# Float16 parts with power-of-two scales in place of float32r parts in a gated MLP

## The chip, the cores and the metric

The kernel runs on one core of a Trainium2 chip. The metric is the device time of one execution in microseconds. Of three runs of the kernel before, the median is 4073.93 us (4071.32 to 4078.27).

## The reference

Three stages follow each other; all data are float32, except that the gated MLP's weights come as float64.

```python
X = np.fft.rfft(x, axis=1)                      # x: 8 sequences x 3072 x 256
Yr = Xr @ w_r - Xi @ w_i + b_r ; Yi = Xr @ w_i + Xi @ w_r + b_i
Y = softshrink(Yr) + 1j * softshrink(Yi)
y = np.fft.irfft(Y, n=3072, axis=1)             # 24576 tokens x 256
z = (sigmoid(y @ w_gate) * (y @ w_val)) @ w_out # 256 -> 1536 -> 256
e = argmax(z @ w_gate8)                         # one of 8 experts per token
out = gate_weight * (relu(z @ w1[e]) @ w2[e])   # 256 -> 1024 -> 256
```

## The kernel before, in words

P1 (lines 84 to 409) transforms one sequence at a time: 256-point transforms as products on TensorE, the 3- and 4-point ones on VectorE (dft3, dft4), the complex mix and the softshrink, and back. The result y goes to DRAM with the features on partitions, in pieces of 128 x 512 (yo, line 406).

P2 (lines 495 to 762) takes y in 48 chunks of 512 tokens, six to a batch (a sequence). A chunk is loaded and split into a high part yhi and a low part ylo (split). A float32 product is made of three products of parts: high by high, high by low, low by high. For each f of 12 groups of 128 hidden features, gvmm issues 12 products of 512 columns into two PSUM tiles gv (six for the gate, six for the value); glu makes the sigmoid (ScalarE), the product p (VectorE), its high part ghi (ScalarE) and its low part glo (VectorE); zmm issues 12 products of 264 columns that add to z (256 outputs, and 8 columns for the choice of the expert, the weights of which prep multiplies into w_out). The z products of a step run behind the gate and value products of the next (pend). There are 48 x 12 = 576 such steps. After 12 of them, route scales the rows of z, chooses the expert and scatters the rows to a table in DRAM.

The parts of y, of p and of the weights are float32r: a high part is a rounded copy, a low part is the rest. The weights arrive as the words of float64 numbers: fetch starts their DMAs once a given value of P1 exists, decode makes float32 of them with integer operations on VectorE and splits them (lines 559 to 584).

The first sequence has the chip to itself. From then on the generator of the next sequence, batch(b + 1), is advanced between the steps of chunk after chunk: nst is the number of its pieces per batch, and they are spread evenly over the first 70 of 72 steps. A list scheduler then sets each engine's order; an engine runs its instructions in that order. Eight products, a maximum and a split for each piece of the experts' weights are woven in the same way (WPrep).

P3 (lines 765 to 994) computes the experts on tiles of 256 sorted rows. Its parts are float16 with a power of two per row and per weight matrix, and again three products stand for one: up (line 918) and down (line 943), each of 256 columns.

## Time and profile before

| | |
|---|---|
| median of three runs | 4073.93 us |
| span of the profiled execution | 4067.2 us |
| TensorE busy | 3994.1 us (98%) |
| VectorE busy | 2443.0 us (60%) |
| ScalarE busy | 1616.1 us (40%) |
| GpSimd busy | 419.6 us (10%) |

For the profiled execution the page gives its span, from the first to the last instruction, and no time around it. A busy time counts each moment once. Products on TensorE overlap, so the mean duration of one is longer than the distance from one to the next; the chain of waits gives a run of products with its count and the time until the next piece, and so their spacing. PE is TensorE's products, PEld its weight loads, DVE is VectorE, ACT ScalarE, POOL GpSimd.

### The profile page before, as it was taken

How to read it: one execution, taken by the hardware profiler on the slowest of the kernel's cores; microseconds unless marked ns; L12 is line 12 of the kernel's file. 1: busy time of each engine (PE TensorE's matmuls, PEld its weight loads, DVE VectorE, ACT ScalarE, POOL GpSimd, SP SyncE). 2: the span in 40 equal slices, each digit the busy share in tenths (PEclk: the TensorE clock that was granted, in tenths of full speed). 3: DMA queues.
4: the chain of work that ended last, by engine and by line, in shares of the span. 5: the costliest groups of instructions: out<-in, count | busy, mean ns of one | idle time of the engine just before them, and what ended most of it. 6: DMA issues, size and time to landing. Idle time of an engine off the chain costs nothing.

```text
span 4067.2 us, 70179 instructions
## 1 busy us (share of the span) xinstructions
PE 3994.1 (98%) x27260; PEld 3533.1 (87%) x27260; DVE 2443.0 (60%) x5820; ACT 1616.1 (40%) x3056; POOL 419.6 (10%) x422
## 2 busy tenths in 40 slices
PE   7899999999999999999999999999999999999998
PEld 5788888888888888888888888888888888888887
DVE  6979768867875886687578568744442222222222
ACT  3545344334544444443344334433333333333332
POOL 1000000000000100000000000000011111111111
PEclk9899999999999999999999999999999999999999
DMA  5311421321252133103101210220032444442442
GB/s 182 112 57 39 143 69 36 108 92 65 68 187 77 68 103 119 37 17 107 42 22 44 87 40 21 85 81 22 11 103 63 122 132 135 132 132 70 116 130 46
DMA packets 289488, 338.00 MB, mean 83 GB/s; under 512 B 153773, under 2 KB 231390, under 8 KB 284928
## 3 DMA queue, kind: packets, MB, share of 16 engines
q1 hardware_dynamic: 267536, 272.70, 23.3%
q0 software_dynamic: 21616, 60.78, 4.2%
q8 instruction: 216, 3.54, 0.4%
q14 instruction: 120, 0.98, 0.1%
HBM read 338.33 MB, written 98.98 MB: 108 GB/s over the span
## 4 chain that ended last, share of the span: by engine, by line
PE 92%; DMA 3%; DVE 2%; issue 2%; ACT 0%; SPq 0%; POOL 0%; POOLq 0%; DVEq 0%; ACTq 0%
PE gv L644 37%; PE zps L671 19%; PE ph L918 12%; PE po L943 12%; PE p1ps L210 5%; PE p1ps L272 2%; DMA u<-A 1%; PE p1ps L394 1%; PE p1ps L194 1%; PE p1ps L393 1%; DMA A<-A 1%; DMA ca<-in_cA 0%; PE eps L943 0%; DMA u<-in_moe_w 0%; PE rps L724 0%
## 5 line engine op out<-in xcount | busy, mean ns | idle before, releaser
L644 PE MATMUL gv<-yhi,w 128*128 128x512 f32 x4608 | 1559.0, 399 | 1.5 <-DVE p L659 1.0
L644 PEld LDWEIGHTS gv<-yhi,w 128*128 128x128 f32 x4608 | 864.6, 188 | 187.5 <-issue 3.0
L644 PE MATMUL gv<-ylo,w 128*128 128x512 f32 x2304 | 909.1, 395 | 0.0
L671 PE MATMUL zps<-w,ghi 128*128 128x264 f32 x4608 | 867.3, 285 | 0.1
L671 PEld LDWEIGHTS zps<-w,ghi 128*128 128x128 f32 x4608 | 751.5, 188 | 49.8 <-ACT ghi L661 0.5
L928 DVE SCALAR_TENSOR_TENSOR hh<-ph,hh 128x512 f16<-128x512 f32 x388 | 268.4, 692 | 731.3 <-ACT hh L927 725.6
L659 DVE TENSOR_TENSOR p<-gv,p 128x512 f32<-128x512 f32 x576 | 396.1, 688 | 487.1 <-PE gv L644 472.6
L671 PE MATMUL zps<-w,glo 128*128 128x264 f32 x2304 | 655.2, 285 | 0.9 <-DVE glo L663 0.9
L658 ACT ACTIVATE p<-gv 128x512 f32<-128x512 f32 x576 | 344.7, 598 | 682.3 <-PE gv L644 661.3
L661 ACT CAST ghi<-p 128x512 fp32r<-128x512 f32 x576 | 357.0, 620 | 588.3 <-DVE p L659 575.4
L943 PE MATMUL po<-wb,hh 128*128 128x256 f16 x4656 | 524.0, 273 | 0.0
L918 PE MATMUL ph<-xT,wb 128*128 128x256 f16 x4656 | 524.0, 273 | 0.0
L943 PEld LDWEIGHTS <-hh 128*128 128x128 f16 x4800 | 470.4, 98 | 59.8 <-issue 4.5
L918 PEld LDWEIGHTS <-wb 128*128 128x128 f16 x4800 | 469.6, 98 | 54.3
L644 PEld LDWEIGHTS gv<-ylo,w 128*128 128x128 f32 x2304 | 433.8, 188 | 78.8
L663 DVE TENSOR_TENSOR glo<-p,ghi 128x512 fp32r<-128x512 f32 x576 | 396.6, 688 | 174.9 <-ACT ghi L661 171.8
L756 POOL DMA_INDIRECT zs<-zr,di x192 | 209.7, 1092 | 2720.8 <-issue 1089.3
L671 PEld LDWEIGHTS zps<-w,glo 128*128 128x128 f32 x2304 | 433.6, 188 | 1.2 <-DVE glo L663 1.1
L927 ACT ACTIVATE hh<-ph 128x512 f16<-128x512 f32 x388 | 232.0, 598 | 283.3 <-PE ph L918 282.5
L953 POOL DMA_INDIRECT out<-ot,tk x200 | 194.9, 974 | 841.6 <-ACT ot L952 832.3
L952 ACT ACTIVATE ot<-po,gs 128x256 f32<-128x256 f32 x194 | 92.1, 475 | 409.1 <-PE po L943 409.1
L210 PE MATMUL p1ps<-wmix,hl 128*128 128x256 f32 x1512 | 196.4, 281 | 0.0
(227 smaller groups left out, 3342.0 us busy)
## 6 DMA issues: line engine op xcount, KB each, us to landing
wb<-wz SPq DMA_DIRECT2D x104, 2048.0 KB
u<-in_moe_w SPq DMA_DIRECT2D x64, 512.0 KB
u<-in_x SPq DMA_DIRECT2D x96, 256.0 KB
y<-yo SPq DMA_DIRECT2D x96, 256.0 KB
y<-y SPq DMA_DIRECT2D x48, 512.0 KB
wz<-u SPq DMA_DIRECT2D x32, 512.0 KB
ca<-in_cA SPq DMA_DIRECT2D x96, 128.0 KB
gc<-in_gC SPq DMA_DIRECT2D x48, 256.0 KB
```

What stands on the lines that cost most here:

```text
L210: nc.tensor.matmul(o, lhsT=lh[:, x, dc], rhs=w[:, wp], start=n == 0, stop=n == 5)
L644: nc.tensor.matmul(ps, lhsT=self.w[f // 4, i, dc][:, wp, f % 4 * 128 : f % 4 * 128 + 128], rhs=yy[:, dc], start=n == 0, stop=n == 5,)
L658: nc.scalar.activation(p, ps[0], AF.Sigmoid)
L659: nc.vector.tensor_tensor(p, ps[1], p, ALU.mult)
L661: nc.scalar.copy(ghi, p)
L663: nc.vector.tensor_tensor(glo, p, ghi.bitcast(F32), ALU.subtract)
L671: nc.tensor.matmul(zps[s][:, : D + NE], lhsT=g[gg][:, sl], rhs=self.w[f // 4, 2, f % 4 // 2][:, f % 2, wp], start=f == 0 and n == 0, stop= ...
L756: i = nc.gpsimd.indirect_dma_start(out=self.zs, out_offset=bass.IndirectOffsetOnAxis(ap=di[:, s : s + 1], axis=0), in_=zw[:, s], in_offset ...
L918: nc.tensor.matmul(ps[:, j], lhsT=w[:, dc * 2 + wp, fc * 128 : fc * 128 + 128], rhs=xT[:, xl * 2 + dc], start=n == 0, stop=n == 5,)
L927: nc.scalar.activation(hh[:, 0, gs2], ps, AF.Relu)
L928: nc.vector.scalar_tensor_tensor(hh[:, 1, gs2], ps, 0.0, hh[:, 0, gs2], ALU.max, ALU.subtract)
L943: nc.tensor.matmul(po, lhsT=hh[:, hl, fc, s * 128 : s * 128 + 128], rhs=w[:, q + wp, k : k + 256], start=n == 0, stop=n == 23,)
```

## The change

The parts in the gated MLP become float16. Before they are split, y is multiplied by a power of two per chunk and the weights by one per matrix. For y, each piece is searched for its largest magnitude as it is written (see); after each third of the inverse transform, of spreads the maximum over the partitions with a transpose and a product and makes the power of two and its inverse. For the weights, wscales does the same over all 18 raw tiles, on the high words of the float64 numbers, before the first is split. The scales are taken out again in the sigmoid's scale, in constants, and in the routing's scales.

```diff
@@ P1.batch, behind the DMA of a piece of y
+                    self.scales.see(q, eh, yf)
                     yield
+            yield from self.scales.of(b, a)
...
+def p2s15(nc, out, P):
+    v = nc.vector
+    v.tensor_scalar(P, P, 16 << 23, 253 << 23, ALU.max, ALU.min)
+    v.tensor_scalar(out[0], P, -1, 268 << 23, ALU.mult, ALU.add)
+    v.tensor_single_scalar(out[1], P, 14 << 23, ALU.subtract)
+
+def spread_max(nc, pool, psum, ident, ones, m, n, name):
+    v = nc.vector
+    ps = psum()
+    nc.tensor.transpose(ps[:n, :128], m, ident)
+    mx = pool.tile([n, 1], F32, tag=name + "x", name=name + "x")
+    v.tensor_reduce(mx, ps[:n, :128], AX.X, ALU.max)
+    dg = pool.tile([n, n], F32, tag=name + "d", name=name + "d")
+    v.tensor_scalar_mul(dg, ident[:n, :n], mx)
+    yield
+    ps = psum()
+    nc.tensor.matmul(ps[:, :n], lhsT=ones[:n, :], rhs=dg, start=True, stop=True)
+    yield ps[:, :n]
+
+class Scales:
...
+    def see(self, q, eh, yf):
...
+        self.nc.vector.tensor_reduce(
+            self.ym[:, q % 2, eh : eh + 1], yf, AX.X, ALU.max, apply_absolute_value=True
+        )
+
+    def of(self, b, a):
...
+        g = spread_max(nc, self.pool, self.pst, self.p2.ident, self.p2.ones, m, 4, "ys")
+        next(g)
+        yield
+        ps = next(g)
+        am = self.pool.tile([128, 2], F32, tag="yam", name="yam")
+        v.tensor_reduce(am, ps.rearrange("p (q h) -> p q h", h=2), AX.X, ALU.max)
...
+        v.tensor_single_scalar(P, P, EXPM, ALU.bitwise_and)
+        p2s15(nc, (sI[:, 0], sI[:, 1]), P)
...
+    def consts(self, c):
+        t = self.pool.tile([128, 4], F32, tag="ct", name="ct", bufs=3)
+        self.nc.vector.tensor_scalar_mul(t, self.p2.kt, self.sc[c][1])
+        return t
...
+    def wscales(self):
...
+        for (q, i, j), t in self.raw.items():
+            n = i * 6 + q * 2 + j
+            h = t.rearrange("p (k t) -> p k t", t=2)[:, :, 1].bitcast(F32)
+            v.tensor_reduce(wm[:, n : n + 1], h, AX.X, ALU.max, apply_absolute_value=True)
...
+        g = spread_max(nc, self.ep, self.pst, self.ident, self.ones, wm, 19, "mw")
...
@@ decode
-            w = self.w[key] = self.wtile(key, [128, 2, 512], F32R)
+            w = self.w[key] = self.wtile(key, [128, 2, 512], F16)
...
-        nc.scalar.copy(hi, Av)
-        v.tensor_tensor(lo, Av, hi.bitcast(F32), ALU.subtract)
+        s = self.sw[:, key[1] : key[1] + 1]
+        nc.scalar.activation(hi, Av, AF.Copy, scale=s)
+        v.scalar_tensor_tensor(lo, Av, s, hi, ALU.mult, ALU.subtract)
...
@@ prep
+        self.wscales()
+        yield
         for q in range(3):
...
@@ split
+        self.yhi = self.yp.tile([128, 2, 512], F16, tag="yhi", name="yhi", bufs=2)
+        self.ylo = self.yp.tile([128, 2, 512], F16, tag="ylo", name="ylo", bufs=2)
+        self.ct[c] = self.scales.consts(c)
+        s = self.scales.sc[c][0]
         for h in range(2):
-            nc.scalar.copy(self.yhi[:, h], self.y32[:, h])
-            nc.vector.tensor_tensor(self.ylo[:, h], self.y32[:, h], self.yhi[:, h].bitcast(F32), ALU.subtract)
+            nc.scalar.activation(self.yhi[:, h], self.y32[:, h], AF.Copy, scale=s)
+            nc.vector.scalar_tensor_tensor(
+                self.ylo[:, h], self.y32[:, h], s, self.yhi[:, h], ALU.mult, ALU.subtract
+            )
...
@@ glu
-        nc.scalar.activation(p, ps[0], AF.Sigmoid)
-        nc.vector.tensor_tensor(p, ps[1], p, ALU.mult)
-        ghi = self.fp.tile([128, 512], F32R, tag="ghi", name="ghi")
+        nc.scalar.activation(p, ps[0], AF.Sigmoid, scale=self.ct[c][:, 0:1])
+        nc.vector.scalar_tensor_tensor(p, ps[1], 2.0**-23, p, ALU.mult, ALU.mult)
+        ghi = self.fp.tile([128, 512], F16, tag="ghi", name="ghi")
         nc.scalar.copy(ghi, p)
-        glo = self.fp.tile([128, 512], F32R, tag="glo", name="glo")
-        nc.vector.tensor_tensor(glo, p, ghi.bitcast(F32), ALU.subtract)
+        glo = self.fp.tile([128, 512], F16, tag="glo", name="glo")
+        nc.vector.tensor_tensor(glo, p, ghi, ALU.subtract)
...
@@ build
-        if k == 55:
+        if k == 34:
             p2.fetch(p1.A[2][:, 0, 0, 0, 0:1])
-    for _ in range(6):
+    for _ in range(7):
         next(prep)
...
-            steps, nst = 0, 118
+            steps, nst = 0, 124
```

The order of TensorE where the first chunk begins. Before, the first two gate and value products (gv, line 644) stand among the inverse transforms of the first sequence (p1ps, lines 397 and 398):

```order
L397 MATMUL p1ps<-gc,u 128x128
L398 MATMUL p1ps<-gc,A_86 128x128
L397 MATMUL p1ps<-gc,u 128x128
L398 MATMUL p1ps<-gn,A_86 128x128
L644 MATMUL gv<-yhi,w_1034 128x512
L644 MATMUL gv<-ylo,w_1034 128x512
L397 MATMUL p1ps<-gc,u 128x128
L398 MATMUL p1ps<-gc,A_86 128x128
```

In the changed kernel, where gv is at line 753, the last inverse transforms (lines 398 and 399) are followed by the pair for the last scale of y (transpose of ym, product with ysd), the pair for the weights (mwm, mwd), and the products that join the expert choice to w_out (lines 705 and 710):

```order
L399 MATMUL p1ps<-gc,A_86 128x128
L398 MATMUL p1ps<-gc,u 128x128
L399 MATMUL p1ps<-gn,A_86 128x128
L453 MATMUL pps<-ident,ym 4x128
L460 MATMUL pps<-ysd,ones 128x4
L453 MATMUL pps<-ident,mwm 19x128
L460 MATMUL pps<-mwd,ones 128x19
L705 MATMUL pps<-ident,u 128x128 x4
L710 MATMUL pps<-wg_481,wt 128x8 x4
L705 MATMUL pps<-ident,u 128x128 x4
L753 LDWEIGHTS w_1142
L753 MATMUL gv<-yhi,w_1142 128x512
```

All gate and value products have moved behind the inverse transforms and the scale pairs.

The order of VectorE in the first sequence's mix. Before, between the values of frequency 128 (h, line 338) and the next dft3 (lines 173 and 174):

```order
L338 TENSOR_TENSOR h_376<-A_85,h_376 128x4
L338 TENSOR_TENSOR h_376<-A_86,h_376 128x4
L313 TENSOR_TENSOR hl<-A_85,hl 128x256
L232 TENSOR_TENSOR A_86<-u 128x4x128
L314 SCALAR_TENSOR_TENSOR hl<-A_85,hl 128x256
L173 TENSOR_TENSOR u<-A_85,A_86 128x516
L174 TENSOR_TENSOR u<-A_85,A_86 128x516
```

In the changed kernel, where these are lines 339, 174 and 175, with the maxima over the raw weight tiles (mwm, line 635):

```order
L339 TENSOR_TENSOR h_379<-A_86,h_379 128x4
L635 TENSOR_REDUCE mwm<-w_441 128x1
L635 TENSOR_REDUCE mwm<-w_443 128x1
L635 TENSOR_REDUCE mwm<-w_445 128x1
L635 TENSOR_REDUCE mwm<-w_447 128x1
L635 TENSOR_REDUCE mwm<-w_449 128x1
L314 TENSOR_TENSOR hl<-A_85,hl 128x256
L635 TENSOR_REDUCE mwm<-w_451 128x1
L233 TENSOR_TENSOR A_86<-u 128x4x128
L315 SCALAR_TENSOR_TENSOR hl<-A_85,hl 128x256
L174 TENSOR_TENSOR u<-A_85,A_86 128x516
L175 TENSOR_TENSOR u<-A_85,A_86 128x516
```

Six of the 18 maxima stand here; two, five and five stand at three other places of the mix.

The order of VectorE in the main loop, near the end of a batch. Before, with p (line 659), glo (line 663), a piece of y (yo, lines 402 and 403) and a maximum for the experts' weights (wm):

```order
L659 TENSOR_TENSOR p<-gv,p 128x512
L663 TENSOR_TENSOR glo<-p,ghi 128x512
L402 TENSOR_TENSOR yo<-p1ps,od 128x2x128
L403 TENSOR_TENSOR yo<-p1ps,od 128x2x128
L402 TENSOR_TENSOR yo<-p1ps,od 128x2x128
L403 TENSOR_TENSOR yo<-p1ps,od 128x2x128
L467 TENSOR_REDUCE wm<-u 128x1
L659 TENSOR_TENSOR p<-gv,p 128x512
L663 TENSOR_TENSOR glo<-p,ghi 128x512
```

In the changed kernel, at such a place (p is line 769, glo 773, yo 403 and 404):

```order
L403 TENSOR_TENSOR yo<-p1ps,od 128x2x128
L404 TENSOR_TENSOR yo<-p1ps,od 128x2x128
L365 MEMSET c_11618 12x2
L475 TENSOR_REDUCE ym<-yo 128x1
L455 TENSOR_REDUCE ysx<-pps 4x1
L457 TENSOR_SCALAR ysd<-ident,ysx 4x4
L769 SCALAR_TENSOR_TENSOR p<-gv,p 128x512
L534 TENSOR_REDUCE wm<-u 128x1
L773 TENSOR_TENSOR glo<-p,ghi 128x512
L488 TENSOR_REDUCE yam<-pps 128x2
L492 TENSOR_SCALAR yam<-yam 128x2
L444 TENSOR_SCALAR yam<-yam 128x2
```

Behind the two instructions of a piece of y now comes its maximum (ym), and behind every fourth piece the chain of a scale (ysx, ysd, yam, then ysc).

## Rows read from the trace of the kernel before

**Rows 1.** Page, busy us of each engine, share of the span, instructions.
```profile
PE 3994.1 (98%) x27260; PEld 3533.1 (87%) x27260; DVE 2443.0 (60%) x5820; ACT 1616.1 (40%) x3056; POOL 419.6 (10%) x422
```
**Rows 2.** Stretches: us, busy PE, PEld, DVE, ACT, POOL, granted clock, DMA, GB/s.
```profile
0.00:141.60 141.60, 96.59 (x525) 76.54 (x526) 105.24 (x257) 54.13 (x97) 15.06 (x30) 0.87 0.53 173
...
1965.49:2325.37 359.88, 359.88 (x2184) 319.26 (x2183) 256.00 (x632) 151.73 (x298) 24.54 (x24) 1.00 0.17 52
...
2997.00:4067.20 1070.20, 1051.82 (x9616) 941.65 (x9614) 306.82 (x663) 336.98 (x610) 198.72 (x204) 0.99 0.40 109
```
**Rows 3.** Waits of PE from 150 to 2985 us: total us, times, longest.
```profile
PE p1ps L394 <- DMA A<-A: 5.3, 7, 1.6
PE zps L671 <- DVE glo L663: 0.9, 1, 0.9
```
**Rows 4.** Chain of waits, last batch: start us, us, run of products.
```profile
2780.28 2.80 PE gv L644 x12
2783.08 1.46 PE zps L671 x12
...
2791.62 1.49 PE zps L671 x12
```
**Rows 5.** Chain of waits in the experts' stage.
```profile
3304.32 5.24 PE ph L918 x48
3309.56 5.24 PE po L943 x48
```
**Rows 6.** Groups, weight loads: count, then busy us and mean ns, idle.
```profile
L644 PEld LDWEIGHTS gv<-ylo,w 128*128 128x128 f32 x2304 | 433.8, 188 | 78.8
...
L918 PEld LDWEIGHTS <-wb 128*128 128x128 f16 x4800 | 469.6, 98 | 54.3
```
**Rows 7.** Groups on DVE and ACT.
```profile
L659 DVE TENSOR_TENSOR p<-gv,p 128x512 f32<-128x512 f32 x576 | 396.1, 688 | 487.1 <-PE gv L644 472.6 <-issue 6.6 <-ACT p L658 5.4
L928 DVE SCALAR_TENSOR_TENSOR hh<-ph,hh 128x512 f16<-128x512 f32 x388 | 268.4, 692 | 731.3 <-ACT hh L927 725.6 <-issue 5.7
L658 ACT ACTIVATE p<-gv 128x512 f32<-128x512 f32 x576 | 344.7, 598 | 682.3 <-PE gv L644 661.3 <-issue 20.1 <-ACT A L279 0.9
L695 DVE TENSOR_REDUCE am<-z 128x4 f32<-128x1024 f32 x48 | 58.3, 1214 | 0.6 <-ACT z L682 0.6
L226 ACT ACTIVATE u<-p1ps,nlam 128x512 f32<-128x512 f32 x12 | 8.2, 688 | 10.9 <-PE p1ps L196 10.9
L434 DVE TENSOR_SCALAR sc<-sc 128x4 int32<-128x4 int32 x48 | 8.0, 167 | 0.0
```
**Rows 8.** Timeline of DVE, two instructions back to back: start us, us.
```profile
59.65 0.69 DVE L173 TENSOR_TENSOR u<-A,A 128x516 f32<-128x516 f32 x1
60.26 0.69 DVE L174 TENSOR_TENSOR u<-A,A 128x516 f32<-128x516 f32 x1
```
**Rows 9.** Chain of waits near 487 us, the routing's small products.
```profile
486.95 0.22 PE rps L724 x2
```
**Rows 10.** Stretches: two chunks; columns as in rows 2.
```profile
330.00:394.90 64.90, 64.90 (x406) 58.33 (x405) 61.23 (x157) 32.10 (x65) 4.60 (x4) 1.00 0.13 41
...
998.40:1062.80 64.40, 64.40 (x402) 57.84 (x402) 56.74 (x143) 33.27 (x62) 6.08 (x4) 1.00 0.22 72
```
**Rows 11.** First stage: timelines of DVE and POOL; waits of DVE before 141.6 us.
```profile
45.79 0.69 DVE L319 TENSOR_TENSOR hl<-A,hl 128x512 fp32r<-128x512 f32 x1
70.87 1.10 POOL L555 DMA_DIRECT2D w<-in_moe_w_gate  x2 [56.01 <-DVE w L552]
...
DVE hl L313 <- ACT hl L311: 5.6, 2, 3.8
...
DVE A L230 <- ACT u L227: 3.9, 2, 3.2
```
**Rows 12.** Chain of waits where the first chunk begins.
```profile
141.85 0.47 PE gv L644 x2
...
146.49 1.16 PE gv L644 x5
```

More of the change, by code (lines that the diff above doesn't have):

```diff
@@ L90, in __init__ @@
         self.psum, self.ps_tag = psum, ps_tag
+        self.scales = None
         self.cp = ctx.enter_context(tc.tile_pool(name="p1c", bufs=1, side="right"))
@@ L405, in batch @@
                         nc.scalar.copy(yo, ps)
[L406 to L408 removed]
+                    yf = yo.rearrange("p j h k -> p (j h k)")
+                    nc.sync.dma_start(out=self.y[b, eh, :, q * 512 : q * 512 + 512], in_=yf)
+                    self.scales.see(q, eh, yf)
                     yield
+            yield from self.scales.of(b, a)
 NE = 8
@@ L436, in p2s, with __init__ @@
     v.tensor_single_scalar(P, P, 1 << 23, ALU.subtract)
+def p2s15(nc, out, P):
[16 more added lines that the diff above has]
+class Scales:
+    def __init__(self, ctx, tc, p2, pst):
+        self.nc, self.p2, self.pst = tc.nc, p2, pst
+        self.pool = ctx.enter_context(tc.tile_pool(name="scl", bufs=1))
+        self.sc, self.ct = {}, {}
+    def see(self, q, eh, yf):
+        if q % 2 == 0 and eh == 0:
+            self.ym = self.pool.tile([128, 2, 2], F32, tag="ym", name="ym", bufs=2)
+        self.nc.vector.tensor_reduce(
+            self.ym[:, q % 2, eh : eh + 1], yf, AX.X, ALU.max, apply_absolute_value=True
+        )
+    def of(self, b, a):
+        nc = self.nc
+        v = nc.vector
+        m = self.ym.rearrange("p q h -> p (q h)")
+        g = spread_max(nc, self.pool, self.pst, self.p2.ident, self.p2.ones, m, 4, "ys")
[4 more added lines that the diff above has]
+        v.tensor_reduce(am, ps.rearrange("p (q h) -> p q h", h=2), AX.X, ALU.max)
+        s = self.pool.tile([128, 2, 2], F32, tag="ysc", name="ysc", bufs=8)
+        sI = s.bitcast(I32)
+        P = am.bitcast(I32)
+        v.tensor_single_scalar(P, P, EXPM, ALU.bitwise_and)
+        p2s15(nc, (sI[:, 0], sI[:, 1]), P)
+        for j in range(2):
+            c = b * 6 + 2 * a + j
+            self.sc[c] = s[:, 0, j : j + 1], s[:, 1, j : j + 1]
+        yield
[3 more added lines that the diff above has]
+        return t
 class WPrep:
@@ L508, in __init__ @@
         self.cp = cpool
-        self.raw, self.w = {}, {}
+        self.scales = Scales(ctx, tc, self, self.pst)
+        self.raw, self.w, self.ct = {}, {}, {}
         self.yp = e(tc.tile_pool(name="yp", bufs=1))
@@ L588, in prep @@
         v = nc.vector
+        self.wscales()
+        yield
         for q in range(3):
@@ L707, in route @@
         ex = ep.tile([128, 2, 4, NE], F32, tag="ex", name="ex")
-        nc.scalar.activation(ex[:, 0], dl, AF.Sigmoid)
-        nc.scalar.activation(ex[:, 1], dl, AF.Sigmoid, scale=-1.0)
+        ct = self.ct.pop(c)
+        nc.scalar.activation(ex[:, 0], dl, AF.Sigmoid, scale=ct[:, 2:3])
+        nc.scalar.activation(ex[:, 1], dl, AF.Sigmoid, scale=ct[:, 3:4])
         t = ep.tile([128, 4, NE], F32, tag="t", name="t")
@@ L750, in route @@
         v.reciprocal(sm, sm)
-        v.tensor_tensor(zw.bitcast(F32)[:, :, D], sm, sc[:, 1], ALU.mult)
+        v.scalar_tensor_tensor(zw.bitcast(F32)[:, :, D], sm, ct[:, 1:2], sc[:, 1], ALU.mult, ALU.mult)
         v.scalar_tensor_tensor(zw[:, :, D + 1], di, 0, self.tok[:, c * 4 : c * 4 + 4], ALU.mult, ALU.add)
```

51 lines of the change are left out of this document (36 added, 15 removed).

## The prediction

> **What bounds the kernel now.** I read the page's busy times first: TensorE is busy for 3994.1 of 4067.2 us, no other engine for more than 60% [rows 1]. Then the busy time by stage. Before 141.6 us the first sequence runs alone, and TensorE is busy for 96.6 us of it; a whole batch of the gated MLP, 360 us, has no gap on TensorE at all, while VectorE is busy for 256 of it; the experts' stage from 2997 us on is as full [rows 2]. The waits of TensorE between 150 and 2985 us confirm it: six groups, of which the reader sees the two largest, sum to 8.5 us [rows 3]. So in the gated MLP, which the change edits, time is what TensorE's instructions take, one after the other, and an edit of the other engines counts only where it makes TensorE wait. In the first 142 us that is the other way round.
>
> **The matrix products.** A step f issues 12 gate and value products of 512 columns, 2.80 us, then 12 products of 264 columns into z, 1.46 us, or 1.49 in some rounds [rows 4]. That is 233.3 and 122 ns each, with float32r operands. The experts' stage shows float16 products with a weight load each, as the change makes them: 48 of 256 columns take 5.24 us, 109.2 ns each [rows 5]. No row shows float16 at 512 or 264 columns, so I bound it. In proportion to 256 columns, 512 take 218.3 ns and 264 take 112.6. If instead a fixed part stands beside the columns, as between float32r's two sizes (slope (233.3 - 122) / 248 = 0.449 ns, fixed part 3.5 ns), then 512 columns take 2 x 109.2 - 3.5 = 214.9 ns and 264 take 112.5. I take 216 and 112.6: the truth should lie between two methods so close. A run of 12 goes from 2.80 to 2.59 us and from 1.465 to 1.35, over 576 steps 121 + 66 us less; with 1.46 as the usual z run it is 63, so 184 us. By the two bounds and the two z runs: 165 to 198.
>
> What could take this back is the weight load. It takes 188 ns beside float32r and 98 ns in float16 [rows 6]. In the experts' stage 98 ns hide under 109 ns, so under 112.6 and 216 they should hide as well.
>
> TensorE gets 24 small pairs more (a transpose of four columns, a product with four columns), three per batch. The nearest row is a float32 pair of the routing, 0.22 us [rows 9]; 24 x 0.2 = 4 us, 3 of each 24 pairs in the first stage. Each second product needs VectorE's maximum and diagonal of the first; the order puts about ten products of the MLP between them in the main loop, which cover two small VectorE instructions.
>
> **VectorE and ScalarE in the main loop.** Replaced instructions cost the same: a scalar_tensor_tensor of 512 columns that writes float16 takes 692 ns, the tensor_tensor 688 [rows 7]. The sigmoid gets its scale from a tile; with an operand from a tile a ScalarE activation out of PSUM takes 688 ns where the sigmoid now takes 598 [rows 7]. These 90 ns lie between the gate's and the value's products, which run 1.3 us apart, so they cost nothing; without that cover they would cost 576 x 0.09 = 52 us.
>
> New on VectorE is a maximum over each piece of y, 96 of 512 columns. A reduction of 1024 takes 1214 ns [rows 7], and back to back an instruction of 516 starts 0.61 us after the one before [rows 8]: 0.61 us each, 12 per batch, 7.3 us, and three chains of eight small ones at about 0.17 us [rows 7], 4 us. Against 360 us this fits. It fits less well by chunk: in the chunk from 330 us VectorE is busy for 61.23 of 64.90 us, and still TensorE has no gap; in the one from 998.4 us for 56.74 of 64.40 [rows 10]. The change makes these chunks 12 x 0.32 = 3.8 us shorter, and nst 124 for 118 brings 5% more background steps into each of the early ones: 61.23 + 0.05 x (61.23 - 12 x 1.38) = 63.5 us of VectorE in 61.1, and 58.7 in 60.6. The first is 2.4 us over, the second fits; the first batch has two such chunks, the others end below the 94% at which TensorE did not wait. I take 4 us. Likewise the seven waits for the copies of A (5.3 us [rows 3]) grow as TensorE reaches those products earlier by some 0.3 us per step in between: 4 us. Together 8, from 0 to 45: the upper end gives each of 21 heavy chunks 2 us.
>
> **The start.** All 18 raw weight tiles must be reduced, spread and turned into scales before the first float16 part is written. The fetch, whose DMAs POOL now issues from 70.87 us on, is moved behind the first correction of the spectral mix, which runs at 45.79 us: some 24 us earlier [rows 11], so the words should be there. The 18 reductions (18 x 0.61 = 11 us) stand between the instructions of the spectral mix. VectorE waits there for ScalarE, 5.6 and 3.9 us in the two largest groups [rows 11]; the first reduction stands behind one short wait of these, so I count 8.5 us of cover and 2.5 us late. Then the order on TensorE matters: now two gate products run already within the inverse transforms and the rest follow from 146.49 us on [rows 12]; after the change all come behind the inverse transforms, behind three scale pairs that stand there without anything between transpose and product (a copy, a maximum over y, two small instructions: some 2 us each, 6 us) and behind the weights' own pair (a dozen small VectorE instructions at 0.17 and a ScalarE cast, 4 us). 2.5 + 6 + 4 and a little queueing behind the decode: 13 us. Bounds: 4 us, if the scheduler's gaps hide all but the last chain; 25 us, if every reduction and small instruction is exposed (30 x 0.61 + 40 x 0.17).
>
> **The sum.** - 184 + 4 + 13 + 8 = - 159 us on the span of 4067.2: 3908. The median of the runs, 4073.93, stands 6.7 us above this span; the page has no other time of the profiled execution, so I add these: 3915 us.
>
> **One rule against the trace.** The rows give nearly the same time per column for both formats: 256 float16 columns in 109.2 ns, 512 float32r columns in 233.3 [rows 4, 5]. The Trainium skill (TensorE: Matmul & The Clock Gate, Back-to-back issue gap) gives a sustained spacing of about 131 ns for 512 columns with a weight load each. By that the gate and value products would lose 6912 x (216 - 131) = 587 us more, and the kernel would take about 3330 us. The trace disagrees: 109.2 ns for half the columns leave no room for 131.
>
> **Rivals.** (a) VectorE becomes the bound of the heavy chunks. For it: 94% without slack in one chunk, and 97% to come in three chunks of each batch. Against it: no wait at that 94%. If VectorE can only be kept 90% busy, a chunk such as that of 998.4 us takes 58.7 / 0.9 = 65.2 in place of 60.6; 21 of them cost 97 us, and the time is about 4000 us. (b) The low side: the start is hidden and nothing waits, at the lower bound of the products: - 198 + 4 + 4, or 3884 us and a little below. (c) Slower than before: the float16 weight load is not hidden in the gated MLP. Place: the 13,824 products of the two groups; price: 13.8 us for each ns that shows; it decides from 12 ns on. With 20 ns exposed the time is 4190 us. For it: in z the load follows a product only 14 ns longer than itself, and the loaded tile was just written. Against it: the experts' second product loads just-written activations at 109.2 ns and shows nothing. (d) The change does not do what it says (float16 products at float32r's pace): 4067 + 6.7 + 25 less what small waits give, no change or slower.
>
> **Chances.** Forecast 0.79 (3880 to 3965, the sum's own bounds: 4067.2 + 6.7 - 198 + 4 + 0 below, and above the start and half of the possible waits at their upper ends: 4073.9 - 165 + 4 + 25 + 25); (b) below 3880: 0.06; (a) 3965 to 4066: 0.09; the page's rule: 0.01; (c) 0.02 and (d) 0.03, of which 0.02 within 0.2%. Less than 0.2%, 8 us, can't be told from no change in this kernel. So faster 0.95, same 0.02, slower 0.03. The range is 3880 to 3965.
>
> **What will show it.** Right: in a chunk of the last batch a gate and value run of 12 in 2.59 us, a z run in 1.35, float16 weight loads near 98 ns, TensorE still without gaps there, the first gate product near 158 us, VectorE above 90% in the first batch's chunks. Wrong: runs above 2.7 and 1.42 us (the price of the products), waits of TensorE for p or glo in the hundreds (rival a), or a first gate product after 170 us (the start).

## The result, and the profile after

The changed kernel takes 3981.57 us (median of four runs, 3979.84 to 3986.95) against 4075.27 us for the kernel before: ratio 0.9775, 95% interval 0.9762 to 0.9789. That is faster, as forecast, but 67 us above the predicted 3915 and 17 us above the range. The profiled span went from 4067.2 to 3978.0 us, 89.2 us where 159 were forecast.

The products do what the prediction said. This is the chain of waits of the changed kernel in the last batch (start us, us, run of products), to set beside [rows 4]:

```profile
2758.86 2.59 PE gv L753 x12
2761.45 1.35 PE zps L781 x12
```

A gate and value run of 12 went from 2.80 to 2.59 us (215.8 ns each), a z run from 1.46 to 1.35. A chunk of the last batch takes 47.65 us where it took 51.67. The weight loads are what [rows 6] let expect; the groups give count, busy us, mean ns and idle time:

```profile
L753 PEld LDWEIGHTS <-w 128*128 128x128 f16 x6912 | 670.3, 99 | 701.5 <-issue 23.2 <-DVE w L686 0.8 <-ACT w L685 0.4
L781 PEld LDWEIGHTS <-ghi 128*128 128x128 f16 x4608 | 450.6, 98 | 185.7 <-ACT ghi L771 0.9 <-issue 0.6
```

What changed is that TensorE now waits. The page's busy times, and the stretches that answer to [rows 2] (us, busy PE, PEld, DVE, ACT, POOL, granted clock, DMA, GB/s):

```profile
PE 3851.4 (97%) x27335; PEld 2758.2 (69%) x27335; DVE 2540.4 (64%) x6166; ACT 1677.8 (42%) x3056; POOL 418.3 (11%) x422
```

```profile
0.00:165.80 165.80, 111.81 (x586) 89.06 (x587) 125.65 (x318) 56.02 (x100) 15.06 (x30) 0.84 0.51 164
1930.00:2274.70 344.70, 340.72 (x2194) 221.72 (x2193) 266.34 (x671) 159.27 (x298) 26.34 (x24) 1.00 0.18 54
2906.80:3978.00 1071.20, 1051.96 (x9620) 941.71 (x9617) 306.97 (x663) 337.47 (x611) 198.73 (x204) 0.99 0.40 109
```

The first stage is 24.2 us longer. The batch in the middle went from 359.9 to 344.7 us, 15 less instead of 24, and TensorE, which had no gap there, is idle for 4 us of it; the experts' stage takes the same time. The seven largest groups of waits of TensorE from 170 to 2900 us (total us, times, longest), to set beside [rows 3]:

```profile
PE p1ps L394 <- DMA u<-A: 13.8, 10, 2.4
PE pps L453 <- DVE ym L475: 8.1, 7, 2.7
PE p1ps L211 <- DVE hl L327: 3.8, 9, 0.7
PE p1ps L395 <- DMA A<-A: 3.7, 4, 1.6
PE pps L705 <- DVE u L676: 3.5, 3, 2.4
PE gv L753 <- DVE p L769: 3.4, 1, 3.4
PE zps L781 <- DVE glo L773: 3.4, 4, 1.2
```

No wait is large. They are of 22 kinds where there were six. Behind the first batch most of them lie in the chunks in which the inverse transform of the next sequence runs: of 38.5 us in batches 1 to 6 the fifth chunks have 23.7, the fourth 7.5 and the third 4.4.

### The profile page after: what moved, and what is told of

Read it like the earlier page. It is cut to its first block, busy times and chain, and to the rows that moved or that the text cites. A ratio compares the mean times of both kernels' runs of the same rounds, so it can differ in the third digit from the quotient of the medians.

```text
span 3978.0 us, 70696 instructions
## 1 busy us (share of the span) xinstructions
PE 3851.4 (97%) x27335; PEld 2758.2 (69%) x27335; DVE 2540.4 (64%) x6166; ACT 1677.8 (42%) x3056; POOL 418.3 (11%) x422
## 4 chain that ended last, share of the span: by engine, by line
PE 78%; DVE 14%; DMA 4%; issue 2%; ACT 1%; SPq 0%; POOL 0%; DVEq 0%; ACTq 0%; POOLq 0%
PE gv L753 28%; PE zps L781 14%; PE ph L1029 13%; PE po L1054 13%; PE p1ps L211 3%; PE p1ps L273 2%; DVE p L769 2%; DVE glo L773 2%; DMA u<-A 1%; DMA u<-in_moe_w 1%; PE p1ps L394 1%; PE p1ps L195 1%; PE p1ps L395 1%; DVE A L184 1%; DVE A L178 1%
## 5 line engine op out<-in xcount | busy, mean ns | idle before, releaser
L753 PE MATMUL gv<-yhi,w 128*128 128x512 f16 x4608 | 1477.5, 381 | 6.0 <-DVE p L769 3.4
L753 PEld LDWEIGHTS <-w 128*128 128x128 f16 x6912 | 670.3, 99 | 701.5 <-issue 23.2
L753 PE MATMUL gv<-ylo,w 128*128 128x512 f16 x2304 | 877.5, 381 | 0.0
L781 PE MATMUL zps<-w,ghi 128*128 128x264 f16 x4608 | 809.7, 276 | 0.0
L781 PE MATMUL zps<-w,glo 128*128 128x264 f16 x2304 | 635.3, 276 | 4.0 <-DVE glo L773 3.4
L769 DVE SCALAR_TENSOR_TENSOR p<-gv,p 128x512 f32<-128x512 f32 x576 | 395.5, 687 | 363.3 <-PE gv L753 349.7
L768 ACT ACTIVATE p<-gv,ct 128x512 f32<-128x512 f32 x576 | 395.3, 686 | 538.2 <-PE gv L753 531.9
L771 ACT CAST ghi<-p 128x512 f16<-128x512 f32 x576 | 354.8, 616 | 564.9 <-DVE p L769 541.8
L781 PEld LDWEIGHTS <-ghi 128*128 128x128 f16 x4608 | 450.6, 98 | 185.7 <-ACT ghi L771 0.9
L773 DVE TENSOR_TENSOR glo<-p,ghi 128x512 f16<-128x512 f32 x576 | 395.6, 687 | 146.3 <-ACT ghi L771 142.5
```

What stands on the lines that cost most here:

```text
L753: nc.tensor.matmul(ps, lhsT=self.w[f // 4, i, dc][:, wp, f % 4 * 128 : f % 4 * 128 + 128], rhs=yy[:, dc], start=n == 0, stop=n == 5,)
L768: nc.scalar.activation(p, ps[0], AF.Sigmoid, scale=self.ct[c][:, 0:1])
L769: nc.vector.scalar_tensor_tensor(p, ps[1], 2.0**-23, p, ALU.mult, ALU.mult)
L771: nc.scalar.copy(ghi, p)
L773: nc.vector.tensor_tensor(glo, p, ghi, ALU.subtract)
L781: nc.tensor.matmul(zps[s][:, : D + NE], lhsT=g[gg][:, sl], rhs=self.w[f // 4, 2, f % 4 // 2][:, f % 2, wp], start=f == 0 and n == 0, stop= ...
```

## The experiments

Seventeen kernels were run, each beside the kernel before on the same chip; a median is that of four runs. Unless the text says so, an experiment is the changed kernel with one edit. "Batches 1 to 3" are the second to the fourth sequence of the gated MLP, "chunk 0" is the first chunk of all. Times of batches and chunks, and sums of waits, come from one profile of each kernel. A wait of TensorE, where I sum waits over a kernel, is an idle time above 0.12 us before a product, counted by how far the distance between two starts exceeds the usual one of the form.

| run | edit | median us | ratio to before, 95% interval |
|---|---|---|---|
| e4_const | all scales constant | 3946.5 | 0.9686, 0.9668 to 0.9704 |
| e5_f32r | scales kept, parts float32r again | 4131.6 | 1.0143, 1.0124 to 1.0162 |
| e1_w_early | weights' scale chain issued earlier | 3969.3 | 0.9751, 0.9727 to 0.9775 |
| f3_w_const | weights' scales constant | 3965.7 | 0.9731, 0.9715 to 0.9747 |
| e2_y_late | y's pairs issued later | 3969.3 | 0.9739, 0.9722 to 0.9755 |
| e3_both_moved | e1 and e2 | 3963.9 | 0.9726, 0.9709 to 0.9742 |
| e7_gap | two empty steps behind the copies | 3982.9 | 0.9777, 0.9761 to 0.9794 |
| f1_three_moves | e1, e2 and e7 | 3962.6 | 0.9719, 0.9701 to 0.9737 |
| f2_late_but_first | f1, first sequence's pairs in place | 3959.2 | 0.9720, 0.9703 to 0.9736 |
| e8_no_glo | no subtraction for g's low part | 3964.6 | 0.9729, 0.9713 to 0.9745 |
| e6_ws_spread | experts' weights two steps per chunk | 3984.6 | 0.9779, 0.9763 to 0.9795 |
| g1_ws_scalar | experts' low part a copy, by ScalarE | 3981.6 | 0.9782, 0.9766 to 0.9798 |
| e9_x_pool | sums of x on GpSimd | 4004.4 | 0.9827, 0.9809 to 0.9844 |
| e10_ws_pool | experts' low parts on GpSimd | 4010.6 | 0.9840, 0.9822 to 0.9858 |
| e11_pool_moved | e1, e9 and e10 | 4005.4 | 0.9823, 0.9805 to 0.9841 |
| h1_ws_queue | experts' loads and stores issued by GpSimd | 4015.2 | 0.9857, 0.9841 to 0.9874 |
| h2_best | f2 and h1 | 3999.8 | 0.9812, 0.9796 to 0.9829 |

### The two halves of the change apart

```diff
# e4_const: no see, no of, no wscales' maxima
+        tc.nc.vector.memset(self.one[:, 0:1], 2.0**15)
...
+            self.sc[c] = self.one[:, 0:1], self.one[:, 1:2]
...
+        for i, e in enumerate((16, 16, 17, 17)):
+            v.memset(s[:, 0, i : i + 1], 2.0**e)
```

> All scales are constants set once (2 to the 15 for y, 16, 16, 17, 17 for the weights): left out are the maxima of y and of the weights, the products and the chains that make scales of them. What stays is the float16 products. If the scales are all that took the gain back (theories P and V alike): first gate product at 140 to 144 us, the whole 3883 to 3900 us (4067.2 - 191 by the paces of the last batch, + 6.7 around the span, + up to 13 for the changes between float32r and float16 products). Theory M (the mixture of float16 and float32r products, or the new order of the steps, costs the rest by itself): 3920 us or more.

```diff
# e5_f32r: yhi, ylo, ghi, glo and the weight tiles
-        self.yhi = self.yp.tile([128, 2, 512], F16, ...)
+        self.yhi = self.yp.tile([128, 2, 512], F32R, ...)
...
```

> Everything of the change stays but the type: y's, the weights' and g's two parts are float32r again, scaled as before by the powers of two, so the order of VectorE, ScalarE and the queues is the changed kernel's, word for word. It prices the additions under the slow products. Theory C (cover): the additions and the copies by DMA are hidden as long as TensorE has 52 us of products per chunk, and stand open only when it has 48: the start is late by the same 20 to 25 us and chunk 0 by 5 to 13, batches 1 to 6 differ from the kernel before by under 4 us each and TensorE's waits there stay under 20 us in all; the whole 4100 to 4130 us. Theory A (the additions cost by themselves, whatever the products): TensorE's waits in batches 1 to 6 are some 45 us as in the changed kernel; the whole 4145 to 4170 us.

With the kernel before and the changed one, these make a table of two by two. It is worked out from the starts of all TensorE products of each profile (us):

| | before | float32r with scales | float16, constant scales | changed |
|---|---|---|---|---|
| first gate product at | 141.6 | 167.6 | 145.2 | 165.8 |
| gate, value and z products at their usual spacing | 2459.3 | 2449.8 | 2269.7 | 2269.7 |
| the same products, time added at the lower clock | 0 | 9.5 | 7.6 | 11.2 |
| other products | 413.5 | 418.9 | 413.8 | 419.8 |
| rest: places where the two kinds meet, small gaps | 7.7 | 19.0 | 13.9 | 15.6 |
| waits | 14.8 | 34.9 | 61.0 | 65.6 |
| experts, from their first product into ph | 1030.3 | 1030.3 | 1030.3 | 1030.3 |
| span | 4067.2 | 4130.0 | 3941.5 | 3978.0 |

The usual spacings of a gate or value product and of a z product are 233.6 and 122.2 ns before, 233.3 and 121.1 in e5, 215.8 and 112.5 in both kernels with float16. The lower clock is told of below.

The fast products alone (third column) shorten the products by 190 us, and the span by only 126: with no scale in the kernel TensorE waits for 61 us. That is theory M's side of e4, and I had expected the other. The scales alone (second column) cost 63 us under the slow products, the median just above the range of theory C and well below that of A: 26 at the start, 20 of waits, 10 at the lower clock. In batches 1 to 6 the waits of e5 are 15 us, as theory C said, but batches 3 and 4 are 6.5 and 4.1 us longer than before, over its 4. The change gains 89 us, where the two halves apart would make 126 - 63 = 63: their costs overlap, the waits (46 and 20 us apart, 51 together) above all.

The clean pair is e5 and the changed kernel. e4 still has the changed kernel's pieces of background (124 per batch), so it differs from the kernel before in order as well as in type. But all five instruction streams of e5, TensorE's, VectorE's, ScalarE's, GpSimd's and SyncE's, have the order of the changed kernel row by row; the type alone takes the waits from 34.9 to 65.6 us, and in batches 1 to 6 from 15 to 39 (before: 6). So most of the waits come with the shorter products. The two largest groups in the main stretch, in e5, then in the changed kernel:

```profile
PE p1ps L394 <- DMA u<-A: 5.7, 5, 1.5
PE pps L453 <- DVE ym L475: 3.5, 4, 1.2
```

```profile
PE p1ps L394 <- DMA u<-A: 11.2, 8, 2.4
PE pps L453 <- DVE ym L475: 8.1, 7, 2.7
```

The copies themselves did not get slower: where TensorE waited for a copy u<-A, its wait ended 5.4 and 5.7 us after the copy was issued in the kernel before, and 4.2 to 6.2 us after in the changed one.

What such a wait looks like without any scale, in e4: the timelines of DVE, then of PE (start us, us; in brackets the idle time before and what ended it):

```profile
1827.64 0.41 DVE L404 TENSOR_TENSOR yo<-p1ps,od 128x256 f32<-128x256 f32 x1
1831.70 0.69 DVE L258 TENSOR_TENSOR u<-u 128x512 f32<-128x512 f32 x1 [3.64 <-DMA u<-in_x]
...
1832.91 0.68 DVE L742 SCALAR_TENSOR_TENSOR p<-gv,p 128x512 f32<-128x512 f32 x1
```

```profile
1833.64 0.38 PE L726 MATMUL gv<-yhi,w 128*128 128x512 f16 x1 [2.98 <-DVE p L742]
```

VectorE's order holds a sum for the next sequence, whose load has not landed, ahead of the p of the present step. VectorE stands for 3.64 us, p comes late, no gv tile is free, and TensorE stands for 2.98.

### The start

```diff
# e1_w_early
-    for _ in range(7):
+        if k == 62:        # before the inverse transforms of the first sequence
+            next(prep)     # wscales
+    for _ in range(6):
         next(prep)
```

> The chain that turns the weight maxima into scales (its two TensorE products among it) is issued ahead of the first sequence's inverse transforms instead of behind them; nothing is left out. Theory P (place): in the changed kernel the last maximum of the weights was there at 101 us, but the product that spreads them stood on TensorE behind the whole first sequence, at 159.85 us, while six half-finished decodes held the buffers u that the inverse transforms need. Then the first gate product comes at 150 to 156 us instead of 165.8, chunk 0 gets back some 8 of its 73.2 us, and the whole takes 3956 to 3967 us instead of 3982. Theory V (VectorE's load): the 115 new maxima of 0.6 us each delay what TensorE waits for, wherever the chain stands; then 3976 to 3984 us.

> The changed kernel with constant weight scales: left out are the 19 maxima of the weights (0.68 us each), their pair and chain; y's scales stay. Theory B (both place and load of the weights' chain delay the start: 18 us got back by the place, which the run with the chain moved showed, and 12 us by VectorE, which that run showed 90% busy from 45 us to the end of chunk 0): chunk 0 ends at 208 to 213 us, whole 3950 to 3958 us. Theory P (place alone): chunk 0 ends at 219 to 223 us, whole 3963 to 3970 us.

The changed kernel's start, in timelines of DVE and PE:

```profile
97.94 3.05 DVE L635 TENSOR_REDUCE mwm<-w 128x1 f32<-128x512 f32 x5
...
165.44 0.74 DVE L686 SCALAR_TENSOR_TENSOR w<-u,mws,w 128x512 f16<-128x512 f32 x1
```

```profile
157.96 0.27 PE L453 MATMUL pps<-ident,ym 128*4 128x128 f32 x1 [1.73 <-DVE ym L475]
159.57 0.35 PE L460 MATMUL pps<-ysd,ones 4*128 4x4 f32 x2 [1.35 <-DVE ysd L457]
159.85 0.28 PE L453 MATMUL pps<-ident,mwm 128*19 128x128 f32 x1
...
165.78 0.63 PE L753 MATMUL gv<-yhi,w 128*128 128x512 f16 x1
```

The last maximum of the weights was there at 101 us. The product that spreads it stands behind the whole first sequence, at 159.85, and the low parts of the weights (L686) come at 165. In e1 that product is at 104.98 us, the first gate product at 144.4 and not at 165.8; chunk 0 itself gets no shorter, against the expectation (76.7 us, 73.2 before the edit), and ends at 221.2 and not at 239.0 (kernel before: 205.7). In f2 and h2 below, whose orders are e1's up to there, chunk 0 ends at 231.1 and 229.6. So the place costs 8 to 18 us at the end of chunk 0; in the medians it is 12, though the intervals of the two ratios touch (0.9727 to 0.9775 and 0.9762 to 0.9789). f3 leaves the weights' maxima out altogether: chunk 0 ends at 220.9, which between such profiles decides nothing, but its median of 3965.7 lies in theory P's range and above theory B's. No cost of the 18 maxima beyond their place is seen, though VectorE is busy for 158.5 of the 176.2 us from 45 us to the end of chunk 0 in e1 and for 147.3 of 175.9 in f3. With y's scales constant as well (e4) chunk 0 ends at 214.1. The three pairs of y in the first sequence stand in TensorE's stream as in the rows for ym and ysd above, with nothing between: about 3.6 us each from the last product before to the next behind.

A second loss was not expected. The granted clock in two stretches of chunk 0 of the changed kernel (columns as in [rows 2]):

```profile
165.80:170.00 4.20, 4.20 (x11) 1.47 (x10) 3.84 (x8) 2.58 (x5) 0.00 (x0) 0.50 0.00 0
...
198.00:202.00 4.00, 3.09 (x13) 2.56 (x14) 1.72 (x5) 2.45 (x4) 0.00 (x0) 0.50 0.02 4
```

Before, TensorE had the full clock from the first gate product to the experts' stage. Now it has 0.50, the lower of its two levels (1.2 GHz), in stretches that follow its pauses: 29 of the 144 gate and value products of chunk 0 stand 427 ns apart in place of 216 and some more lie in between, 7 us more in all.

### The waits behind the first batch

In batches 1 to 7 the waits sum to 10.2 us before, 45.5 after. Three runs move what the largest kinds wait for.

```diff
# e2_y_late: the pairs one and three blocks later
                     self.scales.see(q, eh, yf)
+                    if q % 2 == 0 or eh == 1:
+                        next(self.late, None)
                     yield
-            yield from self.scales.of(b, a)
+            self.late = self.scales.of(b, a, self.scales.ym)
# e7_gap: between the copies by DMA and the inverse products
+                if three and q == 2 * a:
+                    yield
+                    yield
```

> The two small TensorE products per third of a sequence that spread the maximum of y are issued one and three output blocks later (the last third's in the next sequence), and 118 background steps stand in place of 124; all maxima stay, nothing is left out. Theory P: TensorE stands before these pairs because they come right behind the block whose maximum they take (13.3 us before the first products, 6.0 before the second, in 24 pairs after 150 us and some 11 us in the first sequence); moved, they find their input ready: first gate product at 155 to 159 us, waits for ym and ysd under 2 us, whole 3955 to 3968 us. Theory V: VectorE is behind anyway and the waits turn up at the next product that needs it; 3976 to 3984 us.

> Both moves together, nothing left out. Theory P: the first gate product at 141 to 147 us as in the kernel before, chunk 0 near 62 us, no waits for ym, ysd or mwd over 1 us each; the whole 3930 to 3950 us. Theory V: above 3970 us.

> The changed kernel with two empty background steps between the copies by DMA and the first inverse products that read them, in each of the three parts of a sequence (130 steps per sequence in place of 124). Nothing is left out. Theory C (a fixed latency from the last VectorE transform through the copies, no longer covered): TensorE's waits for u and A from DMA in batches 1 to 6 (13.3 us) go to under 4 us and the whole is 8 to 15 us shorter. Theory V (VectorE's load paces these chunks): the waits turn up at other products, within 4 us of the changed kernel.

Waits of TensorE in the main stretch of e3 (pairs moved), then of e7 (copies given time):

```profile
PE p1ps L395 <- DMA u<-A: 11.6, 8, 2.9
PE p1ps L396 <- DMA A<-A: 8.3, 12, 3.3
```

```profile
PE pps L456 <- DVE ym L478: 5.3, 4, 3.7
PE pps L463 <- DVE ysd L460: 5.2, 3, 2.8
PE p1ps L398 <- DMA A<-A: 3.6, 6, 0.7
```

Where the pairs find their input ready (e3), TensorE stands at the copies, for 20 us instead of 13. Where the copies have time (e7), it stands there for 5.5 us and still at the pairs, for 10.5 (before the edit 9.4). The waits of e7 in batches 1 to 7 fall to 37 us, but its gaps under 0.12 us grow by 7 in batches 1 to 6, and the time stays: a sum of waits alone doesn't tell the gain either. e2 and e3 gain about half of what theory P gave. So both were moved together:

> The weights' chain ahead of the inverse transforms, the pairs of y's scale later, and two empty steps between the copies and the inverse products, together (124 steps per sequence). Nothing is left out. Theory X (two kinds of waits, each of which took the other's place when one alone was moved: for the copies and for the pairs): with both moved TensorE's waits in batches 1 to 6 fall from 45 to under 20 us; whole 3935 to 3952 us. Theory Y (VectorE's order is late there in any case; the next product that reads from it waits): waits stay at 35 to 45 us, whole 3958 to 3970 us.

> The same, with the pairs of the first sequence left where they were, since chunk 0 needs the first scale at once. Theory X: chunk 0 ends near 221 us, as with the weights' chain moved alone, and not at 227; whole 3930 to 3948 us. Theory Y: 3955 to 3968 us.

Batches 1 to 7 now wait for 33.8 and 33.1 us: less than 45.5, far from theory X's 20. f2's rows:

```profile
PE p1ps L399 <- DMA A<-A: 5.3, 5, 2.2
PE p1ps L398 <- DMA u<-A: 5.2, 3, 2.3
PE p1ps L212 <- DVE hl L328: 3.1, 8, 0.5
PE zps L791 <- DVE glo L783: 3.0, 3, 1.0
```

f1 and f2 are the fastest versions that compute everything: 3962.6 and 3959.2 us, about 0.55% under the changed kernel by their ratios. In f2 chunk 0 ended at 231.1 us and not near 221, although VectorE and TensorE have e1's order there; so between two profiles the end of chunk 0 can differ by 10 us, and f2 is not to be told from f1. The two profiles differ in the granted clock: 0.88 over the first 221 us in e1's, 0.84 in f2's.

### VectorE's load, and the experts' weights

```diff
# e8_no_glo
-        nc.vector.tensor_tensor(glo, p, ghi, ALU.subtract)
-        return ghi, glo
+        return ghi, ghi
# e6_ws_spread
-            if c > 1 and f % 4 == 1:
+            if c > 1 and f % 8 == 1:
# g1_ws_scalar
-                    v.scalar_tensor_tensor(o[:, 1], t, sc, o[:, 0], ALU.mult, ALU.subtract)
+                    nc.scalar.activation(o[:, 1], t, AF.Copy, scale=sc)
```

> The changed kernel without the subtraction that gives g's low part: left out are 576 VectorE instructions of 0.69 us; TensorE reads the high part in place of the low one, so it multiplies as much as before. Per chunk VectorE has 7 to 8 us less to do. Theory V (VectorE's load in the heavy chunks, 57.6 of 59.6 us in chunk 2 of batch 3, sets what TensorE waits for there and in chunk 0): waits in batches 1 to 6 go from 45 to under 20 us, chunk 0 from 73 to about 66 us, the whole -30 to -50 us. Theory C (latency of copies and of pairs that stand in order): under -15 us.

> The changed kernel with one edit: the preparation of the expert weights advances two steps per chunk in place of three, so that it ends in the sixth sequence and not in the fourth. Same work, nothing left out. Theory W: batches 1 to 3 lose more than batches 4 to 6 (344.7, 350.2, 351.9 us against 343.2, 344.6, 341.0) because VectorE, in order, stands behind ScalarE and the loads of this preparation (one stand of 4.1 us in chunk 4 of batch 3); then batches 1 to 3 get back 8 to 15 us, batches 4 and 5 lose up to 4, the whole -5 to -12 us. Theory C: what counts is the transform's own chain, within 4 us of the changed kernel.

> The changed kernel in which ScalarE writes the expert weights' second part as a copy of the first; left out is the subtraction on VectorE (32 instructions of 1.28 us in sequences 1 to 4) that gives the low part. ScalarE has 32 passes more. Theory W (VectorE, in order, stands there behind ScalarE and the load of a weight, and what is behind it in its order comes late to TensorE: the run with the slower preparation showed the loss moving from batch 2 to batch 4 with it): batches 1 to 3 (344.7, 350.2, 351.9 us) come to 341 to 345 each, the whole 10 to 20 us under the changed kernel's 3982. Theory Q (the loads of the preparation are ahead of the transform's copies in SyncE's queue, so that the copies land late): batches 1 to 3 stay within 3 us each, the whole within 6 us.

e8 leaves out 576 instructions of 0.69 us on VectorE (395 us) and gains 17 us, between the two theories. Chunk 0 gets 7.6 us of it (73.2 to 65.7), as theory V said; behind the first batch the waits only fall from 45.5 to 40.0. There VectorE's load is not what TensorE waits for. In e6 the loss moves with the preparation of the experts' weights (batch 2 from 350.2 to 345.6 us, batch 4 from 343.2 to 351.7), but the sum stays. In g1 VectorE no longer takes part in the second half of that preparation: batches 1 to 3 take 347.0, 351.4, 350.2 us, as before the edit, and VectorE then stands for ScalarE instead (glo for ghi, up to 5.2 us at once). Theory W falls.

### Work and transfers given to GpSimd

```diff
# e9_x_pool
-                nc.vector.tensor_tensor(xf[:, 0], xc[:, 0], xc[:, 1], ALU.add)
+                nc.gpsimd.tensor_tensor(xf[:, 0], xc[:, 0], xc[:, 1], ALU.add)
# e10_ws_pool
-                    v.scalar_tensor_tensor(o[:, 1], t, sc, o[:, 0], ALU.mult, ALU.subtract)
+                    nc.scalar.activation(t, t, AF.Copy, scale=sc)
+                    nc.gpsimd.tensor_tensor(o[:, 1], t, o[:, 0], ALU.subtract)
# h1_ws_queue: WPrep's three dma_start
-            nc.sync.dma_start(out=t, in_=src)
+            nc.gpsimd.dma_start(out=t, in_=src)
```

> The changed kernel with the sums and differences of the two halves of x (72 and 72... in all 84 instructions of 0.69 us on 128 by 512 numbers in sequences 2 to 8) on GpSimd in place of VectorE. Nothing is left out. Theory S (stand in order): in chunks 4 and 5 VectorE's order holds these sums of the next sequence ahead of the sigmoid product p, the blocks yo and the maxima ym; where the load of x lands late (3.6 us in one place of the run with constant scales) VectorE stands, and TensorE behind it, for gv or for ym. Then the long waits at the end of chunk 4 (2.0 us at 1860.8, 2.7 us at 2203.8) go, TensorE's waits in batches 1 to 6 fall from 45 to 25 to 35 us, and the whole is 8 to 20 us shorter than the changed kernel's 3982. Theory L (VectorE's load alone, 0.69 us times 12 per sequence): 3 to 6 us shorter, long waits stay. Against both: the sums take longer on GpSimd and the transform that reads them comes late; then slower.

> The changed kernel with the low parts of the expert weights (32 VectorE instructions of 1.28 us) on GpSimd, after one more ScalarE pass each that scales the weights in place. Nothing is left out. Theory S: VectorE no longer stands behind ScalarE and the loads of that preparation (up to 4.1 us at once in chunk 4 of batch 3): batches 1 to 3 (344.7, 350.2, 351.9 us) come to 342 to 347 each, the whole 6 to 15 us shorter. Theory L: 41 us of VectorE's work gone in the first four sequences, of which a tenth shows: 2 to 5 us. Against both: ScalarE's added pass delays the sigmoid.

> Both of these and the weights' chain issued ahead of the inverse transforms (as in the run that moved it alone, which took 12 us off). Nothing is left out. If the three are independent: 3982 - 12 - 8 to 20 - 6 to 15, 3935 to 3956 us by theory S; by theory L 3959 to 3965 us.

> The changed kernel with the loads and stores of the expert weights' preparation issued by GpSimd in place of SyncE; the work on the engines is the same, nothing is left out. Theory Q (the loads stand in SyncE's queue among the transform's copies, so that the one or the other lands late and an engine that works in order stands): batches 1 to 3 (344.7, 350.2, 351.9 us) get back 3 to 8 us each, the whole 8 to 20 us under 3982. Theory E (the engines' own in-order work of that preparation, wherever it is queued): within 5 us of 3982.

> The same queue, with the weights' chain ahead of the inverse transforms, the pairs of y's scale later (but for the first sequence) and two empty steps behind the copies, which together took 3959 us. Theory Q: 3940 to 3952 us. Theory E: 3955 to 3965 us.

By their medians all five are 23 to 41 us slower than the version that they were built on, and no theory's range was met. What was seen in e9 and e10 is in the last section. In h1 batches 1 to 3 take 357.0, 357.5 and 360.3 us: VectorE waits up to 5.9 us at once for the weights' loads, 3.1 in the changed kernel. So these runs don't tell whether the shared queue of SyncE is at fault.

## Why the prediction was wrong, step by step

**The products: right.** - 184 was predicted; by the table the products take 190 us less, by the last batch's chunks 48 x 4.02 = 193. (Redone with the terms as they stand, the prediction's bounds are 167 and 208 in place of 165 and 198; the measured values lie within both.) Neither rival (c) (weight loads exposed) nor the 131 ns for 512 columns that the Trainium skill gives (TensorE: Matmul & The Clock Gate, Back-to-back issue gap) is seen: 215.8 ns, with loads of 98 hidden.

**The pairs: + 4 predicted, + 6 measured** (other products, 413.5 to 419.8).

**The start: + 13 predicted, + 24 measured**, still within the bounds of 4 to 25. The three pairs of y and the weights' pair were named, but taken at 2 us and 4; the rows show about 3.6 us for each pair of y, and 6 from the weights' product to the first gate product. That the chain could have gone ahead of the inverse transforms was not asked. With 11 us for the three pairs and 6 for the weights', 7 remain: some 4 are there in e4 too, without any scale (145.2 for 141.6), and 3 I cannot place. The first gate product at 165.8 lies between the 158 and the 170 of the prediction.

**The main loop: + 8 predicted, from 0 to 45; this is the step that failed.** The waits grew by 51 us (14.8 to 65.6). The step priced two causes, VectorE's load in two chunks (4 us) and seven copies that TensorE reaches 0.3 us earlier (4 us). It took the absence of gaps in the trace of before for room. Of the 51 us, 9 lie in chunk 0, where TensorE waits for the preparation of the weights, 6 in the rest of the first batch, 32 in batches 1 to 6 and 3 in the last. For the 32 the runs showed something else than the two causes: VectorE, ScalarE and the copies by DMA, each in a fixed order, carry the transform of the next sequence in chains that the faster products do not shorten, while TensorE's work that covered them got 8% shorter. What was "no gap" in the trace of before was a chain that just fitted. e4 shows it with no scale in the kernel (46 us of added waits in all), e5 and the changed kernel with the same order (31 us from the type alone, 23 of them in batches 1 to 6). That it is the cover is the reading of these sums; no run lengthened TensorE's work alone under float16. Rival (a) named the place, the heavy chunks, but the wrong cause: VectorE's load. e8 took 7 to 8 us per chunk of it away and the waits behind the first batch fell by 5.5.

**Two terms that the prediction didn't have: 11 and 8 us.** The gate, value and z products lose 11.2 us at the lower clock, which before they never met; 7 of these are in chunk 0. And the rest (7.7 to 15.6 in the table) grows by 8. It is not the meeting of float32r with float16: e5, with float32r alone, has the largest rest, 19.0, and where TensorE goes from gate, value or z products to others and back without a wait, the mean time above the usual spacings is - 3 ns before and 9 ns in the changed kernel, 3 us over its 317 such places. What the other 5 us are made of is not separated.

The sum of the measured terms, 24.2 - 189.6 + 11.2 + 6.3 + 7.9 + 50.8 + 0 (experts), is the measured - 89.2. The 6.7 us that the prediction added around the span are 1.8 for the profiled execution after (3979.84 to 3978.0); the other 5 are the spread between runs.

**The checks.** VectorE above 90% came out in the third to fifth of the first batch's six chunks (96, 95 and 92%); the others stand at 84, 68 and 70%. The fourth chunk (columns as in [rows 2]), for the first of [rows 10]; it holds 439 products where it held 406, so its length is no measure of the waits:

```profile
358.00:425.40 67.40, 65.81 (x439) 44.95 (x438) 64.33 (x165) 36.83 (x71) 5.79 (x4) 1.00 0.13 40
```
That TensorE has no gaps in the last batch held for five of its six chunks; in the last it waits for 3.4 us where it waited for 1.0.

**What stays open.** Of the waits behind the first batch 12 us went when pairs and copies were both given time; with the pairs alone moved the waits for the copies grew. Which chain would be the last if all were moved was not found; the loss goes with the preparation of the experts' weights in some batches, through VectorE, ScalarE or the loads, and no run separated these.

## What to carry to other kernels

A full engine without gaps shows that everything else just fits, and not how much room it has: before making it faster, read what each background chain (engine order, copy, product) takes from end to end in the heaviest stretch, and set it against the shortened cover, since a busy share of 90% or of 75% on the other engine decides little. A reduction that feeds a scale has its place in the in-order stream of the engine that spreads it: look for the last operand's time and for the place of the product that uses it. One wait moved away is no gain until the whole time has fallen: the same time can come back as another wait, or as many small gaps.

## What the runs showed of the hardware

GpSimd work is not free beside VectorE. In e9 the 84 sums of x left VectorE (84 x 0.69 = 58 us), and still the page reads:

```profile
PE 3854.4 (96%) x27335; PEld 2756.2 (69%) x27335; DVE 2545.9 (64%) x6082; ACT 1676.5 (42%) x3056; POOL 538.4 (13%) x506
```

VectorE is busy for 5.5 us more than in the changed kernel. 53 of its instructions are stretched by more than 0.3 us, 51 us in all; in the changed kernel none is. One of them, with what GpSimd does meanwhile:

```profile
1281.17 3.52 DVE L773 TENSOR_TENSOR glo<-p,ghi 128x512 f16<-128x512 f32 x1 [0.68 <-issue]
```

```profile
1280.65 0.97 POOL L867 DMA_INDIRECT zs<-zr,di  x1 [0.30 <-issue]
1281.63 1.28 POOL L258 TENSOR_TENSOR u<-u 128x512 f32<-128x512 f32 x1
1282.86 1.28 POOL L259 TENSOR_TENSOR u<-u 128x512 f32<-128x512 f32 x1
```

An instruction of 0.69 us ends 0.55 us after the second sum of GpSimd. Of the 38 instructions that read gv and p (L769) while one of these sums ran none took longer than 0.69 us; of the 28 of L773 (glo), whose two operands both lie in SBUF, 17 were stretched. The Trainium skill (SBUF — State Buffer, SBUF: two separate sides) says that VectorE and GpSimd share a pair of ports as an exclusive lock, which a VectorE instruction with two SBUF operands needs beside a GpSimd one that reads SBUF, and that the loser blocks fully. The trace agrees, with 3.52 us in place of 0.69, and in that each of the 53 began while a GpSimd instruction was running; some small instructions with one operand were stretched too, which this does not sort. In e10 24 instructions of VectorE are stretched, by 33 us. That these stretches make the whole 23 and 29 us slower is likely and not shown by itself.

TensorE pays for some pauses twice. Behind its waits of 2.4, 2.7 and 3.4 us (at 1471, 2204 and 2895 us of the changed kernel) six gate and value products follow at 427 ns each, 1.3 us more per wait, and in chunk 0 it is the 7 us told above. Behind the one at 2203.75, with the columns of [rows 2]:

```profile
2203.70:2206.00 2.30, 2.25 (x15) 1.70 (x15) 1.43 (x4) 0.62 (x1) 0.00 (x0) 0.79 0.25 87
2206.00:2208.40 2.40, 2.40 (x7) 0.89 (x8) 2.23 (x8) 0.00 (x0) 0.00 (x0) 0.50 0.00 0
2208.60:2211.00 2.40, 2.40 (x18) 1.55 (x16) 0.69 (x1) 0.90 (x2) 0.00 (x0) 1.00 0.00 0
```

The clock (the last column but two) falls to the lower level here after TensorE has started again (0.79 in the first row) and is back in the third row; at the other two waits it fell about when TensorE started. Not every such pause did this: behind the 2.98 us shown for e4 the granted clock stayed at 1.00.

An activation of ScalarE with its scale from a tile takes 686 ns where the plain one took 598 [rows 7], as foreseen; it cost nothing that can be seen, since the waits of TensorE for the sigmoid's p are 2.5 us in all from 170 to 2900 us.
